# Retuning the order tables of a fused attention and gated MLP kernel: new tables, moved branch hints, a pinned instruction stream and five split stores

## The chip, the cores and the metric

The kernel runs on one core of a Trainium2 chip. The metric is the device time of one execution in microseconds. Before the change three runs took 411.26, 409.59 and 414.25 us, median 411.26 us. The engines are named as in the profile: PE (TensorE), PEld (its weight loads), DVE (VectorE), ACT (ScalarE), POOL (GpSimd) and SP (SyncE, which issues the DMAs here). A name with a q behind it (SPq, PEldq) stands for an engine's sequencer: instructions that aren't counted as busy.

## The reference

Attention over 4 batches, 8 heads, 768 positions, head size 64, with a linear bias per head, a mask that keeps the first 8 keys and the last 96, and then a gated MLP with a mixing step over positions:

```python
scores = scale * np.matmul(q, k.transpose(0, 1, 3, 2)) + bias
scores = np.where(keep, scores, -1000000000.0)     # keep = is_global | is_local
a = softmax(scores);  x = a @ v                    # (B, S, H * D)
h = gelu_tanh(x @ w_in);  u, v = h[..., :512], h[..., 512:]
v_n = (v - mu) / np.sqrt(var + 1e-06) * g_ln
v_s = np.einsum('ts,bsd->btd', w_sg, v_n) + b_sg[None, :, None]
out = x + (u * v_s) @ w_out
```

## The kernel before

**Units.** Attention is cut into 48 units (batch, pair of heads, third of the positions). A unit's work is: load q and k, and v; the scores on PE (line 1104, tile s_ps); bias, maximum, exponential, sum and scaling on DVE, ACT and POOL (lines 1136 to 1166); turning p over; p·v on PE (line 1253, tile av); copying the result to x as a high and a low part. The first 16 units are turned by PE transposes (line 1225, tile tps). From unit 16 on, `turn_blocks` turns them by DVE block transposes (line 1192) and two trips through DRAM: four DMAs far<-tt (line 1200), then one DMA pt<-far (line 1204), which the p·v of that unit waits for.

**MLP.** All MLP matmuls run as three products of high and low parts (lines 570 to 572, tile mm_ps, 128x384 or 128x512 columns). The last batch's output product is done with seven instead of eight block products (`seven`, lines 813 to 815, with DVE sums at line 825 and POOL or DVE sums at line 706). The outputs of the other batches leave by `out_tile`: DVE sum (690), a second sum (692), one store of 128x384 (694).

**Who sets the order.** All these steps are recorded as ops of a `Plan`. Each op may have several ways, that is engines that can run it. Two long strings steer the planner: a digit of `SHIFTS` for each op moves it earlier or later, and a letter of `WAYS` (P, D, A, or - for free) ties it to an engine. `Plan.order` replays the program with a table of costs, and `emit` (line 512) then writes the instructions, each engine's in that order. [...] The planner also knows that PE's instructions come in blocks (`BLOCK, FIRST_BLOCK, FETCH = 256, 194, 4.6`), and where it expects PE to wait early on, `keep_on` (line 507) puts in dummy matmuls on a tile of zeros (line 510, tile on).

**The end.** When all is done, every engine loads a flag (`nc.values_load`, line 1569, TENSOR_LOAD) and branches over a long general path (line 1570, COMPARE_BRANCH) that isn't taken with these inputs. `HINTED` (line 51) names, for DVE and for PE, how many of its ops from the end a BRANCH_PREFETCH_HINT for that branch is put. SP then collects the landings of all stores, and the engines meet at line 1715.

Of the kernel before, what the change touches and what calls it, by code (L numbers as in the profile page):

```python
# [19 lines left out]
P = 128  # L20
B, H, S, D = 4, 8, 768, 64
# [29 lines left out]
HINTED = ("DVE", 40, mybir.EngineType.DVE), ("PE", 14, mybir.EngineType.PE)  # L51
# [12 lines left out]
    "030E00HNf0wWo3NQSa0-F000J3V00-0q00E60u1CCqxzqNK7BSfs0-ebeTiQzPqGhdhU28O-x9np3k-lf-dk-L--HXk9WBg-Mb0OO686YQM1"  # L64
    "e0h0P-yqd---qS8kaDFR5ZV-eCzM-2k04uLgcSrldkZ000q7A00cB00enHlh30xr9cgM-N-OqKsPCYw8qkp0PZy9nokS-R414k0ykpsPavC-"
    "0UfU-JH6Kt-WgQfH1X0gy-yf-jVQd-8NdvjBNKSHS-3982BA7-vDa3Ch2LEFE0rnq2DUFbslTJV4q00t0FMhne9zYT7el9Mty--T1nN-TvLb"
    "NiN0S5m3spkyhWa06hMX07l92859IJH-E-TGd7vZ2i8HVXE8aVdHeVJ4Rhoq61qH9UMyLetgskrIMJe0O-4c0f3n0L5vbOESgBUTarmu49IX"
    "AiWBkaoZ-Twt20X5H7oSiK--0ZAwjXgCndju-YZea--T-P-Zzx7K-O-wCqnwZp0elG7U0e1F0Z7058RnsbddzcHGqRC0l-q0eFCHY1qGiHUn"
    "GQN6Rc1ikjo010KY40V-nWqBOk2WF-S0M6PN08BO0GP1o0vc86-WNa8pfMsSNRG8uqGuEYfaUTok-Kn5GNl8PFtdPcc07q-l4GcgGVsd8-Oy"
    "rsYcaVH2p0900ii0Fj0r00ZIRVy-1-nJ-X1KtksqNrR0SyRfarGro3Zj0SKTNE-wW0JChQOXh-EZ-qA8lTK-H-Rn--0pMBN0a0aLQSuuOBs-"  # L70
    "4U9xGMirD6BR-4FJNxurbhkVT5Y7fiOj2xhlW7CWOs4bTgL3ZMI0WI7ZX04ZCLo5Qy1Tj0wFTqtqfe1Wd0--hv--zcImzro-YZLNQ00YSueM"
    "afZLL-04sOTYHrAGQkMHqhFMvDsud3g0G10rYbouGmZIRsl-aOdDbf9kflwaRmjGGQA4e-fd-YMcgneL--W-zss2yfS03nIrylMX-0XQ03-0"
    "wvFjLmutx-0dIqPJ00fSCE505qlt97zTzcHhTIl77QcSMW6-Tb8SfkCfA-S800mVD8X-cnFZ-HOS-IiSlDpxpFoZQFaRKi-YpwpwIe0fBj2g"
    "08ECdU7OsN40MZpZWn90F10stNQzT3G347V9EZJl0Z00E-DfrD0GQ6pj098kCRliAN-sj3x99nsNmSN40iCEIojpq0nNsjnlFJt006KoCTvP"
    "ZRsC-50UvSAQ8u-nVv-Tp6tiFHtVc0QRk92PTl0C0tOhCjuu0tZ2U0blHB59-H2WXtVucGK--6QoYmqouuyhnppJrra08MLlUBXIIvYD5P0u"
# [12 lines left out]
    "0E2Dun7WTXgBwwkpCGyd"
# [3 lines left out]
    "----P------------P--DA--DD-----------DDA---D----D----------DPA----D--P-ADAD-A-A--------D-DADD--P--D-------DD"  # L92
    "P-------------D-AA-P--P--AD----P--DP----A----------DPAP--P--A--------A--------------A-DDP---D--AD--------P--"
    "-A-D--D-D----------P-A------AD--------DDPDD--D----------P---PA--P--AD--------D-P----A--DDP-P-A----------P--P"
    "P---P------------DADPD----D--------P---DA--D--A----------P-----P--APD-A-A--------D-DPA------DD-----AD-------"
    "---A--A----------P---AA-----AD--P--AD--------D-D------A-D--A-D----------AAPA-P----------P-D----A----------A-"
    "A--P-----------A------A-A-PP-A-D--------P---AA-P------------AD--D--P-----------ADD----------A-D-------------"
    "----AA-P---A--------P-P--P--D--AD------P--D--PD------D------------P-D---------------P-P-----A---P--D--------"
    "--P---AP--D---D--D--PD-P--AP-------------------------A-------------ADD---------A---PP--P-PD-AD-DP-----------"
    "D------D------D------P---------A-ADPDDD--------P-PADD-----------------------AAPPDD--------A-DDDP--DD--------"  # L100
    "-------------D-A---D---------P-A-AP---PDP--------------------------P-A----D--------D--AA---------D--DPP----P"
    "DP-------DPD---------------A-D-A---------D-P-AD----------AD-D----------P-D-----P------------AP--------------"
    "----------A-----------A-PADA----------PPD-----------D-------D-----------D-P-----P---------------------------"
    "----A--D----------A--D-P-----------D-----------DAP-----------------------PPP----------------DD--------------"
# [174 lines left out]
class Plan:  # L279
# [233 lines left out]
    def emit(self, start):  # L513
# [10 lines left out]
        for o in todo:  # L524
# [3 lines left out]
            if o.quarters is not None:  # L528
                self.keep_on(o)
# [1189 lines left out]
```

## Time and profile before

| | |
|---|---|
| three runs, us | 411.26, 409.59, 414.25 |
| the profiled execution, us | 412.14, of which 410.4 us from first to last instruction |
| PE busy | 396.4 us, 97% of the span, 4628 matmuls |
| DVE busy | 349.2 us, 85% |
| ACT, POOL busy | 222.3 us, 54%; 209.4 us, 51% |
| DMA | 67.14 MB, 164 GB/s over the span |

Busy PE isn't PE at its peak: its matmuls overlap, so one that is listed with 0.33 us follows the one ahead by about 0.17 us where nothing holds it. The rows further down are given as the trace's views print them: groups of waits (who waited, for whom, total us, times, longest), timelines (start, duration, engine, line, operation, tiles, and in brackets the idle time ahead and what ended it), single lines of the program with their sequencer instructions, and DMA queues of a stretch.

### The profile page before, as it was taken

To read this page: it belongs to the slowest core of one execution; us is meant where nothing else is said; L and a number is where in the kernel's file an instruction comes from. 1 tells how busy PE (TensorE), PEld (TensorE's weight loads), DVE (VectorE), ACT (ScalarE), POOL (GpSimd) and SP (SyncE) were. 2 spreads that over 40 slices of the span, in tenths; PEclk is the share of its full clock that TensorE was granted. 3 is DMA by queue.
4 is the path that set the end of the run, shared out by engine and by line. 5 is a ranking of instruction groups with operands and counts; after the bars stand their busy time and mean duration, and the time that the engine had idled before them with its cause. 6 is when DMAs were issued, how large, how long until landed. Compare 5 with 4: busy or idle time off the path is not lost.

```text
span 410.4 us, 12613 instructions
## 1 busy us (share of the span) xinstructions
PE 396.4 (97%) x4628; PEld 362.7 (88%) x4630; DVE 349.2 (85%) x1151; ACT 222.3 (54%) x733; POOL 209.4 (51%) x336
## 2 busy tenths in 40 slices
PE   7889999999899999999999999999999999999993
PEld 4777777999799898999999988999999888999993
DVE  7899999999998999987768899986767768796894
ACT  5899999875544777643344575752343324241300
POOL 4434887875544472753121453726113534785780
PEclk9999999999999999999999999999999999999997
DMA  7864765536887787838398566617284641000013
GB/s 244 281 188 145 222 201 149 165 92 176 242 245 262 208 259 199 271 96 260 100 269 270 182 149 197 192 46 227 72 267 106 190 149 58 2 1 2 1 38 122
DMA packets 50035, 67.14 MB, mean 164 GB/s; under 512 B 5808, under 2 KB 33968, under 8 KB 49968
## 3 DMA queue, kind: packets, MB, share of 16 engines
q1 hardware_dynamic: 49968, 66.28, 52.8%
q8 instruction: 38, 0.62, 0.7%
q14 instruction: 29, 0.24, 0.2%
HBM read 47.91 MB, written 18.35 MB: 161 GB/s over the span
## 4 chain that ended last, share of the span: by engine, by line
PE 80%; DVE 10%; DMA 4%; ACT 2%; issue 1%; POOL 1%; SPq 0%; DVEq 0%; ACTq 0%; POOLq 0%
PE mm_ps L570 22%; PE mm_ps L572 21%; PE mm_ps L571 21%; PE av L1253 7%; PE s_ps L1104 6%; DVE p L1136 2%; PE tps L1225 2%; ACT p L1141 1%; DMA pt<-far 1%; DMA far<-tt 1%; DMA stage<-in_w_out_dram 1%; DMA qk<-in_qk_in_dram 1%; DVE win L932 1%; PE mm_ps L815 1%; PE mm_ps L814 1%
## 5 line engine op out<-in xcount | busy, mean ns | idle before, releaser
L1141 ACT ACTIVATE p<-p,pst 128x168 f32<-128x168 f32 (+1 forms) x192 | 80.7, 422 | 34.8 <-DVE pst L1136 30.2
L570 PE MATMUL mm_ps<-wsg,z 128*128 128x384 f32 x192 | 64.9, 338 | 0.0
L572 PE MATMUL mm_ps<-wsg,z 128*128 128x384 f32 x192 | 64.3, 335 | 0.0
L571 PE MATMUL mm_ps<-wsg,z 128*128 128x384 f32 x192 | 64.2, 334 | 0.0
L1163 POOL TENSOR_SCALAR p<-p,pst 128x168 f32<-128x168 f32 (+1 forms) x89 | 39.6, 455 | 36.8 <-DVE pst L1154 30.1
L1136 DVE CUSTOM_DVE_ANT_0 p<-s_ps,bias 128x168 f32<-128x168 f32 (+1 forms) x192 | 54.5, 318 | 4.4 <-PE s_ps L1104 3.2
L1253 PE MATMUL av<-pt,v 64*64 64x128 f32 (+1 forms) x1408 | 48.9, 252 | 4.2 <-DMA far<-tt 1.6
L1253 PEld LDWEIGHTS av<-pt,v 64*64 64x64 f32 x1408 | 37.3, 133 | 13.6 <-issue 7.3
L570 PE MATMUL mm_ps<-x,win 128*128 128x384 f32 x128 | 43.7, 341 | 0.0
L572 PE MATMUL mm_ps<-x,win 128*128 128x384 f32 x128 | 42.9, 335 | 0.0
L571 PE MATMUL mm_ps<-x,win 128*128 128x384 f32 x128 | 42.8, 335 | 0.0
L1104 PE MATMUL s_ps<-qk 64*64 64x64 f32 (+2 forms) x1408 | 39.1, 243 | 0.2 <-DVE vg L592 0.2
L570 PE MATMUL mm_ps<-win,x 128*128 128x512 f32 x96 | 39.2, 408 | 0.0
L572 PE MATMUL mm_ps<-win,x 128*128 128x512 f32 x96 | 37.7, 393 | 0.0
L571 PE MATMUL mm_ps<-win,x 128*128 128x512 f32 x96 | 37.6, 392 | 0.0
L570 PEld LDWEIGHTS mm_ps<-wsg,z 128*128 128x128 f32 x192 | 36.0, 188 | 1.3 <-issue 0.8
L1104 PEld LDWEIGHTS s_ps<-qk 64*64 64x64 f32 x1408 | 34.7, 137 | 2.6 <-issue 1.0
L1141 ACT ACTIVATION_READ_ACCUMULATOR p<-p,pst 128x1 f32 x192 | 36.4, 189 | 0.0
L571 PEld LDWEIGHTS mm_ps<-wsg,z 128*128 128x128 f32 x192 | 36.1, 188 | 0.2
L572 PEld LDWEIGHTS mm_ps<-wsg,z 128*128 128x128 f32 x192 | 36.0, 188 | 0.0
L587 ACT ACTIVATE u<-mm_ps 128x384 f32<-128x384 f32 x32 | 15.6, 488 | 36.5 <-PE mm_ps L572 36.1
L570 PE MATMUL mm_ps<-gt,wout 128*128 128x384 f32 x96 | 32.8, 342 | 0.0
(194 smaller groups left out, 997.6 us busy)
## 6 DMA issues: line engine op xcount, KB each, us to landing
qk<-in_qk_in_dram SPq DMA_DIRECT2D x32, 328.0 KB, 4.5
pt<-far SPq DMA_DIRECT2D x24, 384.0 KB, 4.2
v<-in_v_in_dram SPq DMA_DIRECT2D x32, 256.0 KB, 4.0
out_dram<-o SPq DMA_DIRECT2D x28, 192.0 KB, 3.7
far<-tt SPq DMA_DIRECT2D x52, 96.0 KB, 3.0
qk<-in_qk_in_dram SPq DMA_DIRECT2D x16, 276.0 KB, 3.5
far<-stage SPq DMA_DIRECT2D x44, 96.0 KB, 1.9
v<-in_v_in_dram SPq DMA_DIRECT2D x16, 192.0 KB, 4.0
```

The lines of the kernel that those rows point to most:

```text
L570: mm(ps.ap, ah, bh, start=(i == 0), stop=False)
L571: mm(ps.ap, ah, bl, start=False, stop=False)
L572: mm(ps.ap, al, bh, start=False, stop=(i == n - 1))
L587: op([on_act(n) + (lambda: nc.scalar.activation(out.ap, h.ap, AF.Square, scale=math.sqrt(GELU_C * GELU_A)),)], [h], [out])
L814: mm(ah, bl, start=False, stop=False)
L815: mm(al, bh, start=False, stop=r == 1)
L1104: nc.tensor.matmul(s_ps[h][e * HQ:(e + 1) * HQ, i * W + c0:i * W + c0 + n], qk[rows, qc:qc + HQ], qk[rows, QW + k0:QW + k0 + n], start=Tru ...
L1136: nc.vector.tensor_tensor_reduce(out=p[:, g, cols], in0=s_ps[h][:, i * W:i * W + nk], in1=bias[:, 2 * j + h, w0:w0 + nk], op0=ALU.add, op1 ...
L1141: op([on_act(nk, 0.225) + (lambda p=p, g=g, cols=cols, i=i: nc.scalar.activation(p[:, g, cols], p[:, g, cols], AF.Exp, bias=st[:, 0, i, g: ...
L1163: op([on_pool_ts(nk) + (partial(scaled, lambda o, a, c: nc.gpsimd.tensor_scalar(o, a, c, 1.0, ALU.mult, ALU.mult)),), on_act(nk, 0.13) + ( ...
L1225: nc.tensor.transpose(tps[:, a * P:(a + 1) * P], pc[:, c:c + P], ident)
L1253: nc.tensor.matmul(to, v[rows, vc:vc + D], of, stop=True, skip_group_check=True, **kw)
```

## The change

The two tables are replaced whole. The hints move from 40 to 100 ops before the end on DVE and from 14 to 16 on PE. Ahead of PE's 87th op (counted from 0: `o.place == 86`) an address directive makes the loader pad PE's stream so that the next instruction stands in slot 232 of a 256-slot block; the padding is branched over. Five stores of the third batch (4 of its second half, 1 of its first) are issued as two DMAs of 64 rows each.

```diff
-HINTED = ("DVE", 40, mybir.EngineType.DVE), ("PE", 14, mybir.EngineType.PE)
+IN_TWO = {(B - 2, NCH - 2, KD - 1)} | {(B - 2, NCH - 1, m) for m in range(KD)}
+HINTED = ("DVE", 100, mybir.EngineType.DVE), ("PE", 16, mybir.EngineType.PE)
+ALIGNED = 86, 232
...
 SHIFTS = (
-    "030E00HNf0wWo3NQSa0-F000J3V00-0q00E60u1CCqxzqNK7BSfs0-ebeTiQzPqGhdhU28O-x9np3k-lf-dk-L--HXk9WBg-Mb0OO686YQM1"
+    "LJ0b0XJM0eA0ccV3WXFtrkNLJPNBzF-FhqNNAe2a0eJXbD0C201PKrBnf-6J1QojnW2wfVKTvELgvf1avq45VV30K18Hwfz2OkO5b0dc00ZN"
...
 WAYS = (
-    "----P------------P--DA--DD-----------DDA---D----D----------DPA----D--P-ADAD-A-A--------D-DADD--P--D-------DD"
+    "-----P-D---------D-D-----D---------P-DD-A-DD--A--------------AP----D-D-DAP----A----------PPD-------D------DD"
...
         todo = self.search(start)
+        for i, o in enumerate([o for o in todo if o.quarters is not None]):
+            o.place = i
...
             if o.quarters is not None:
+                if o.place == ALIGNED[0]:
+                    nc.tensor.addr_align(256, offset=ALIGNED[1], max_nops=0)
                 self.keep_on(o)
...
-    def out_tile(self, x, c, m, dst):
+    def out_tile(self, x, c, m, dst, parts=1):
...
-            op([("SP", 0.42, 0.7, lambda: nc.sync.dma_start(dst[ms, cs], o.ap))], [o], [])
+            def store():
+                for h in range(parts):
+                    rows = slice(h * P // parts, (h + 1) * P // parts)
+                    nc.sync.dma_start(dst[m * P + rows.start:m * P + rows.stop, cs], o.ap[rows])
+
+            op([("SP", 0.42, 0.7, store)], [o], [])
...
-                   [[moe.out_tile(x, c, m, dst) for m in range(KD)] for c in range(NCH)])
+                   [[moe.out_tile(x, c, m, dst, 1 + ((b, c, m) in IN_TWO)) for m in range(KD)] for c in range(NCH)])
```

The arithmetic is the same: PE has the same 1620 MLP matmuls, 704 score and 704 p·v products and 88 transposes in both programs, and 105 dummies instead of 106. The line numbers of the changed program are 6 to 11 higher (570 becomes 576, 825 becomes 836, 706 becomes 717).

**First place: PE, the first p·v that is fed through DRAM** (unit 16, tile pt of the far path; x and win are the operands of an MLP product of the v half). Before:

```order
L570 MATMUL mm_ps_1956<-x_989,win_332 128x384
L571 MATMUL mm_ps_1956<-x_989,win_332 128x384
L572 MATMUL mm_ps_1956<-x_989,win_332 128x384
L1253 MATMUL av_2066<-pt_2005,v_1844 64x128
L1253 MATMUL av_2068<-pt_2005,v_1844 64x128 x2
```

Changed:

```order
L576 MATMUL mm_ps_2052<-x_991,win_333 128x384
L577 MATMUL mm_ps_2052<-x_991,win_333 128x384
L578 MATMUL mm_ps_2052<-x_991,win_333 128x384
L1264 MATMUL av_2075<-pt_2006,v_1812 64x128
L1264 MATMUL av_2077<-pt_2006,v_1812 64x128 x2
```

The same p·v follows an MLP product in both, but it has moved six MLP matmuls back: between it and the p·v of unit 15 stood 45 of them and now stand 48, and three more stand ahead of that one (78 for 75).

**Second place: DVE, its last work before the flag is loaded** (o and kept are output tiles of the last batch, mm_ps the last products). Before:

```order
L825 TENSOR_TENSOR o<-x,mm_ps 128x384
L706 TENSOR_TENSOR o<-o,x 128x384
L825 TENSOR_TENSOR o<-x,mm_ps 128x384
L706 TENSOR_TENSOR o<-o,x 128x384
L825 TENSOR_TENSOR kept<-kept,mm_ps 128x384
L1569 TENSOR_LOAD general
```

Changed:

```order
L836 TENSOR_TENSOR o<-x,mm_ps 128x384
L717 TENSOR_TENSOR o<-o,x 128x384
L836 TENSOR_TENSOR kept<-kept,mm_ps 128x384
L836 TENSOR_TENSOR o<-x,mm_ps 128x384
L717 TENSOR_TENSOR o<-o,x 128x384
L1580 TENSOR_LOAD general
```

PE's last product fed `kept`, which takes one DVE instruction; it now feeds an `o`, which takes two.

**Third place: PE, the hint for the branch at the end.** Before:

```order
L572 MATMUL mm_ps_6262<-wsg_1382,z_5928 128x384
L1715 BRANCH_PREFETCH_HINT
L813 MATMUL mm_ps_6052<-x_6240,late_5931 128x384
L814 MATMUL mm_ps_6052<-x_6240,late_5931 128x384
L815 MATMUL mm_ps_6052<-x_6240,late_5931 128x384
```

Changed:

```order
L578 MATMUL mm_ps_6272<-wsg_1381,z_5820 128x384
L1726 BRANCH_PREFETCH_HINT
L576 MATMUL mm_ps_6272<-wsg_1381,z_5937 128x384
L577 MATMUL mm_ps_6272<-wsg_1381,z_5937 128x384
L578 MATMUL mm_ps_6272<-wsg_1381,z_5937 128x384
```

Counted over PE's stream (a weight load and a matmul for each product, scores and p·v issued twice, semaphore waits one each), the hint stood 87 instructions ahead of the branch and now stands 98 ahead. On DVE it stood 49 ahead and now stands 123 ahead.

## Rows read from the trace of the kernel before

**Rows 1.** The page: busy us and share by engine; one instruction queue (packets, MB, share).
```profile
PE 396.4 (97%) x4628; PEld 362.7 (88%) x4630; DVE 349.2 (85%) x1151; ACT 222.3 (54%) x733; POOL 209.4 (51%) x336
...
q8 instruction: 38, 0.62, 0.7%
```

**Rows 2.** Windows: busy us of PE, PEld, DVE, ACT, POOL; clock, DMA share, GB/s.
```profile
100.00:110.00 10.00, 8.37 (x105) 7.91 (x104) 8.86 (x30) 5.72 (x20) 2.67 (x4) 1.00 0.88 264
...
350.00:360.00 10.00, 10.00 (x59) 9.96 (x58) 8.22 (x18) 2.74 (x5) 7.57 (x10) 1.00 0.01 2
```

**Rows 3.** Waits of PE (first, second and last of nine rows).
```profile
PE av L1253 <- DMA far<-tt: 1.6, 1, 1.6
PE av L1253 <- issue: 1.3, 1, 1.3
...
PE s_ps L1104 <- DVE vg L592: 0.2, 1, 0.2
```

**Rows 4.** Timeline of PE around 104 us.
```profile
104.02 0.34 PE L572 MATMUL mm_ps<-x,win 128*128 128x384 f32 x1
105.99 0.68 PE L1253 MATMUL av<-pt,v 64*64 64x128 f32 x24 [1.63 <-DMA far<-tt]
```

**Rows 5.** Timeline of SP's DMA issues, 94 to 101 us.
```profile
94.75 1.79 SPq L1200 DMA_DIRECT2D far<-tt  x4
96.64 2.72 SPq L913 DMA_DIRECT2D stage<-in_w_out_dram  x3
99.68 0.33 SPq L1204 DMA_DIRECT2D pt<-far  x1
```

**Rows 6.** Timeline of PE around 17 us.
```profile
17.12 0.43 PE L1253 MATMUL av<-pt,v 64*64 64x128 f32 x2 [1.26 <-issue]
```

**Rows 7.** Chain of waits, a stretch of attention: start, us, engine, tile, line.
```profile
200.09 1.06 PE av L1253 x48
201.15 1.18 PE s_ps L1104 x64
```

**Rows 8.** Timeline of the end.
```profile
403.13 0.56 DVE L825 TENSOR_TENSOR o<-x,mm_ps 128x384 f32<-128x384 f32 x1
...
403.73 0.56 DVE L706 TENSOR_TENSOR o<-o,x 128x384 f32<-128x384 f32 x1
403.73 0.34 PE L815 MATMUL mm_ps<-gt,wout 128*128 128x384 f32 x1
404.20 0.55 DVE L825 TENSOR_TENSOR kept<-kept,mm_ps 128x384 f32<-128x384 f32 x1
```

**Rows 9.** Line 1570, the branch: ns min/median/max, first and last start us.
```profile
L1570 SPq EVENT_SEMAPHORE  x8: 17/17/17, 405.7 to 408.2; - x8
...
L1570 DVEq COMPARE_BRANCH  x1: 84/84/84, 404.7 to 404.7; - x1
L1570 SPq COMPARE_BRANCH  x1: 53/53/53, 405.2 to 405.2; - x1
L1570 PEldq COMPARE_BRANCH  x1: 3664/3664/3664, 405.6 to 405.6; - x1
L1570 DVEq EVENT_SEMAPHORE  x1: 21/21/21, 408.0 to 408.0; - x1
```

**Rows 10.** Line 1715, hint and closing of the program, the same columns.
```profile
L1715 SPq EVENT_SEMAPHORE  x10: 17/28/825, 408.2 to 410.3; - x10
...
L1715 PEldq BRANCH_PREFETCH_HINT  x1: 45/45/45, 393.8 to 393.8; - x1
```

**Rows 11.** DMA from 393.8 to 405.6 us, its only instruction queue.
```profile
q14 instruction: 2, 0.02, 0.4%
```

**Rows 12.** DMA from 405 to 408.2 us: PE's instruction queue; last store's landing.
```profile
q8 instruction: 1, 0.02, 2.2%
...
out_dram<-kept SPq DMA_DIRECT2D x1, 192.0 KB, 3.0
```

**Rows 13.** DMA from 400 to 404.7 us: landing of the store of kept before it.
```profile
out_dram<-kept SPq DMA_DIRECT2D x1, 192.0 KB, 2.0
```

More of the change, by code (lines that the diff above doesn't have):

```diff
@@ new lines @@
+    "MZWw9n4-oUxuckTXWIeThmq5IKlV-50O4VtS-j0dmo94U2mZ000JHtHns-xfD4QQ67J64jZ0F57R00w4vodyM8eh09s0Do35X4F16SE1ntVO"
+    "E-u4KT46E5V0ZUb8woA8RJU6RMrB0Vup-Z6rQ80doSPV5ur----8--yTKZ-t---n--v2BBt7oj00000Y4R5m5hNUzCuRldRjts7x-g-yT-nv"
+    "9iQ1WZku8ml8bnSe0LswyuV0z1--l7y--C2mg--M5q--pWcx9i9V04iBLAzpTIE0Pb16sjtanFsWclFX9GLMHSZEJJKgGdI5k2-Rtjk84hMy"
+    "Nr5-sPpQ-75vtIGtFFTtUrxdGbrY-KYrfadRvcS8rqlWGiWDDU3bJRJL5qz0bvcvvxxaDrt3PFRDAtRuupblR-vJQJ7uFRrmXd00M3eWtF2f"
+    "1p1L23GVp18LmG4Ys1OccgKJ-h1-RBC16u8f3Y1Y-bDM-67ER5PZSI0NhhBDSRC9w3Q6aagO9l-Scgpw-Lj8YCw1crW1wl-eKRq7-sQeRx5m"
@@ new lines @@
+    "lFGV0ayIU5NIsUa4XNtouxHb-X0Kd3510YAcf6NB69jpSJW-smSAw0g0awTSdOVzdAZ49eaQYVaFFF68EeJYH-ubr0Bd0XWca0g-I9-F0-13"
+    "16P04LPKt0w0FG160wsfiUuT-k-k7eGgZW-lcDTj8u-6qi9M3QY1F0Qlm0LoO0005038BzvdGsvT450-t--Zr--f---y-y-V-qjdUsONBnS3"
+    "G9dWv-c9fU-mW0l6TlptOJX3NR-d-Oa-9NkWAOeKA6DBBgL4AABDAkFG4WpyGwaocSO-esWFHQ0O8Dccnk04rlQzmHWhYQUz-S8U0BHU07yK"
+    "3krSIbGr--B7Okc-zdywZf0Z004kkA9WykrfGAfcWeWPL5Fm0OMVntcDhr069fJXhwosU2o0nxT9M9Yzrz-P-UzVfYdcvJL1CCG-1NSrOTvr"
+    "d-UJshGqmYK6vJ-0Lv00f1PmjjImM1OoNNe7Bh8CJnCd0okgfs3h80Osh100nilYA9Cc7A-6bYWRMgF0SiUFBePOyz-w-qrnJFr--O-M7Xhj"
@@ new lines @@
+    "sUIhtF5FiG7F0T0wFt-vyWQa2Nq6skk30907DS2v09Og595u0FMa06ym8MkGj5GVKtBpvaQaXEsyTTUO80-tucRXtf9P430-7H1F-Aa90k0R"
+    "f88Z-WwNGp---tPqbo-----5WomDz--8jCMP7CSyMvUYOccyudtpidAJcFdEUpWdbLMBgDtbo-fgdXEc0Ft-5FcU0fylFQ5-Z-vhl---f---"
+    "maHh000qvp7XuSs00MFWpv3c60uj4zoNAhllFQiGeCIf7LEM3fSBGNYE3aX9E00cnV9-8n-PViI4LfA9oUQwsfLK1Gu69XJLez-100UUVSg0"
+    "kfhetJ2V0t2aSiT0gvtR--zq-I-s--Rt-C8Y5T-7jPpDxxJqYDVkXS4bkuR7203c--bKsnje9aeSgHHSNm0vK03452G50N3lDQoCnPWR8nvC"
+    "gr30ezB-8d7Bv01S0oXFQW00MaDnPIsdr-rYSsdUS4ajTCY5XmVe--vks6WglA0-ym-lO0c0ymoAzVV1PRTL-0N831c-kFnW79N9aNrR0FqA"
@@ new lines @@
+    "5H9o7fKNaMfJMDHVS00AaEUW9-6QSIaWe0i2XrVracVWKgYoIQJZ070TyywyyWbmBQxyA-lVD-5af2U5k0q50010aZee0ejFjNbLGy77kSHF"
+    "7M11zEBd9CNjDH6KwLEKtG6Rp-L5-z26kI4J70SE1JU50s20P0eTE8SowcRo-rr-z-oz-EcOUYS-1Ix0IKlR6G4-BqlLWcP-C0Td1RPp000p"
+    "UhEOr5gqeFG4urFP00YOOZ2glpPsO6S0hH4ilc5a4h5Glzlw-w---NaWDx---vWUfj--jgB--o85M8T78--jhf72PW9Xk0saVT91LJobMO5u"
+    "BGTxIV-MvCCUMO5PFdCPhXW-CftbZd55N7977QMfiDQocd0B0SEQPCnwAGstW8gKtft3ptE7hHN8ezE-jUbrkIvi6HfRX0LFycVaJFfC-CTI"
+    "dkknY8ndEP1Yt0MkLtb0ahHVpsxN8sy8Zbg65AG-r7Ie-I-s6PS2p-0cRUOaW5S2-cbguayZH828d1Fj---yXt--bU9X5jmAF--c0DviNbNe"
@@ L89 @@
+    "Uu-VGwkZO-L-EII-UeGSLd0S6pps-MdaRMbJJ-UKf02902bv-Z67vOBH0bHuzuvrZYmKpmKbnWyQs0xCxEWh5lFcHLE0X2V8K5A29308qGEu"
+    "i087I-Q7j-Z7PdxtSt1alYoBiUa4ZElKzmIS0IKTW0pk9UOSO0vfKNiR7T-IcmTGxuC0jbukopGLeofaeWEWZMbsWsH00000-nG0Db0008lC"
+    "kyQarbqijX5u9PFqWJuSlbBMlVl4I1BkJttKO2BQHMhJ3oNxu8YCgKIBG005JNHEcxt9GabMMLnHq20xlaakpx3T8TwFK3yDbO-lxf54UytL"
+    "-G4V7OYo-eTvzcFMsY-Z"
 )
 WAYS = (
[L92 removed]
@@ L117 @@
+    "-P--P-PP---P-D-----------------------P-----------------DPPD---------------DAD---------------D-DD---P---P----"
+    "-----------DDDD-DDA--------D---------------D-DPAP-A------------D---D--------P--DD-------PDPP-D--------------"
+    "-----D----D---------"
 )
```

69 lines of the change are left out of this document (21 added, 48 removed).

## The prediction

> **What bounds the kernel now.** I began with the page. PE is busy for 97% of the span and nothing else is above 85% [rows 1], so the question is where PE's missing time lies, and what stands behind its last matmul. The windows answer the first half: from 110 us to the end of the matmuls PE has no idle stretch worth naming, and a typical window, 350 to 360 us, holds 59 matmuls in 10.00 us, one per 0.17 us, at the full clock [rows 2]. The one bad window behind the start is 100 to 110 us, with 8.37 us busy. The waits of PE name it: nine rows, 7.4 us in all, the largest a p·v that waits 1.6 us for the trip through DRAM, then 1.3 us in which PE waited for nothing but its own instructions [rows 3]. The timeline shows the first: a matmul starts at 104.02, the p·v of unit 16 at 105.99 [rows 4]. SP had put three weight loads between the four DMAs out (94.75) and the one back (99.68) that fills its tile [rows 5]. The second lies at 17.12 us, in dense attention [rows 6].
>
> The end is the other place. The last matmul starts at 403.73 and DVE is done at 404.75 [rows 8], yet the span is 410.4 us. The rows of line 1570 say why: PE's branch, which should take tens of ns, took 3,664 ns, and DVE, whose branch was over at 404.8, did nothing until 408.0 [rows 9]. SP spent 825 ns of its closing sequence on the last arrival, PE [rows 10]. PE's instruction queue moved 38 packets of 16 KB for some 9,260 matmuls and weight loads, about 250 instructions each [rows 1]; none of them came between the hint at 393.8 [rows 10] and the branch at 405.6 [rows 11], and one came right behind the branch [rows 12]. So the hints of the old program prefetched nothing; DVE's was no better.
>
> **The change part by part**, against the profiled run's 412.14 us (410.4 us of span and 1.74 around it; it lies 0.88 above the median 411.26, and I move the sum over to the median at the end).
>
> *PE's own work* is unchanged: same matmuls, one dummy fewer. Changes between quarter-array and whole-array matmuls go from 40 to 42; both new ones are in the first 30 us, where dummies fill PE's waits. 0.0.
>
> *The wait at 104 us.* Six more MLP matmuls stand ahead of this p·v, 6 x 0.17 = 1.0 us of work that used to come behind the wait. SP's rows there keep their order (four DMAs out, three weight loads, one back) and DVE has one instruction fewer ahead of the second block transpose, so the landing hardly moves. I take -1.0. Bounds: 0 if the landing slips as far, -1.6 if the wait goes whole [rows 4].
>
> *The other waits of PE* (7.4 less these 1.6, less 1.3 for instructions and 1.0 for the first tile of zeros) come to 3.5 us; the 1.1 us for the first softmax stays, since the order there is the same. Every engine's order around the others is new. They could go (-2.4), or a new one could come as long as the longest row (+1.6) [rows 3]. With no row for the new order I take 0.
>
> *The alignment.* PE meets one branch over some 70 pads, at a place ahead of a group of dummies. A branch whose target is at hand costs SP 0.5 us from its start (405.2) to the next instruction (405.7) [rows 9]; behind waiting dummies that is hidden. 0, at most +0.5. It also moves the block edges of all that follows; see the third rival.
>
> *The split stores.* Five more DMA issues on SP of 0.3 us each, at about 345 to 370 us, where the DMA share is 0.01 [rows 2] and SP only waits for the next output. No load is queued behind them. 0; if the buffers came free 0.4 us later, no PE op would see it there.
>
> *The hints.* PE's stood 75 instructions ahead of its last block edge (counted at 194 + 256k, which puts the idle time of [rows 6] at the 450th instruction, on an edge) and is now 8 ahead of it, with 90 more to the branch; the old branch came 12 behind its edge. DVE's stood behind its last edge and is now just ahead of it. If the target is fetched when the edge frees a block, PE's 3.66 us go. But DVE's and PE's late arrival cover each other and the last store: it landed 3.0 us after its issue [rows 12], where the one of the same size before it took 2.0 [rows 13], and SP's closing could start no earlier. What PE alone adds is SP's 825 ns less the usual 28 [rows 10]: -0.8, taken. Bounds: 0 if the hints still miss; -1.9 if, with no fetch in its way, the last store also lands 1.0 us sooner, plus a tenth from the next arrival.
>
> *The tail.* PE's last product now feeds an o tile instead of kept, two DVE instructions instead of one. In the trace such a pair starts at 403.13 and 403.73, 0.60 apart, and ends 0.56 later; the single one takes 0.55 from 404.20 [rows 8]. DVE would end at 404.20 + 0.60 + 0.56 = 405.36 instead of 404.75, and the last store, the flags and the branches with it: +0.6. Nothing covers it.
>
> Sum: -1.0 - 0.8 + 0.6 = **-1.2 us**, 410.9 for the profiled run, **410.1 us** against the median.
>
> [...] The rows show a branch that waited 3.66 us for its target in spite of a hint [rows 9]. [...]
>
> **The rivals.**
> 1. *The hints miss again.* For it: neither old hint brought a packet in, and PE's too had an edge between it and the branch [rows 10 and 11]. Against it: the old edge lay only 12 instructions ahead of the branch. The end then keeps its 3.66 us: -1.0 + 0.6 = -0.4, 410.9 us.
> 2. *The waits ahead of 110 us go, and the last store lands early.* -1.6 - 2.4 - 1.9 + 0.6 = -5.3, 406.0 us. For it: all of it is in the list of waits. Against it: the order of every engine is new there, and what makes one wait go can make the next.
> 3. *Slower: PE outruns its instruction fetch at a moved edge.* Attention matmuls run at 1.18/64 us (scores) and 1.06/48 us (p·v) each [rows 7], two of each to a product. Between two edges near 200 us the changed stream now holds 27 score products, 32 p·v products and 6 MLP matmuls: 1.0 + 1.4 + 1.0 = 3.4 us, with the changes of array shape 3.7. Before, the shortest block behind the start held 32, 24 and 14: 1.2 + 1.1 + 2.4 = 4.6 us, and PE showed no idle time there. A fetch asked for on arrival took 3.66 us [rows 9]. So this block stands at the point where it decides: a fetch slower than about 3.7 us stalls PE. One more block, near 295 us, has 32, 25 and 11: 4.2 us. If both stall like the one at 17 us, 1.3 each [rows 6], the forecast becomes -1.2 + 2.5 = +1.3, 412.6 us.
>
> **How the numbers follow.** Forecast 0.45 (410.1, by its own bounds 408 to 412), rival 1 0.25 (410.9), rival 2 0.13 (406.0), rival 3 0.17 (412.6). The predicted time is the forecast's, 410.1. The range: the first two cases lie within 408 to 412.5, rival 3 with one more wait of 1.0 reaches 413.4, and half of rival 2 comes in at 407.0; beyond these ends I leave about 2 in 10. One per cent is 4.1 us, about what separates a change from none in runs that spread from 409.59 to 414.25; below 407.1 lies most of rival 2 and a little of the forecast's tail, 0.14; above 415.4 only rival 3 with a new wait of 1.6 and more, 0.06; the rest, 0.80, is within 1%.
>
> **What would show it.** In the changed profile: PE's COMPARE_BRANCH well under 1 us and an instruction packet between its hint and its branch (else rival 1); the idle time ahead of the first p·v from DRAM at about 0.6 us instead of 1.63; DVE's last pair ending about 1.3 us after PE's last matmul ends; PE's "issue" row no longer than 1.3 us in all (rival 3 shows as PE idle on "issue" near 200 and 295 us). The forecast is wrong if new waits of over 1 us stand in PE's list, or if the last matmul doesn't start within 402 to 404 us.

## The result, and the profile after

The changed kernel takes **406.92 us** (median of 6 runs, 406.4 to 409.24) against 411.72 us for the kernel before (6 runs, same chip): ratio 0.9895, interval 0.9849 to 0.9942, 4.3 us by the ratio. That is just below the low end of the range (407.0) and 3.2 us below the predicted time. The profiled execution of the changed kernel took 406.97 us, its span is 405.2 instead of 410.4.

The 5.2 us of span lie in two places: the last matmul starts at 400.23 instead of 403.73 (-3.50), and the stretch from there to the end is 4.96 instead of 6.63 us (-1.67). First PE. The page (busy us, share, instructions), and the windows of [rows 2]:

```profile
PE 396.0 (98%) x4629; PEld 362.8 (90%) x4629; DVE 345.5 (85%) x1149; ACT 224.9 (56%) x736; POOL 198.9 (49%) x335
...
q8 instruction: 38, 0.62, 0.7%
```

```profile
100.00:110.00 10.00, 10.00 (x114) 9.58 (x113) 9.51 (x35) 5.45 (x23) 4.13 (x5) 1.00 0.81 259
...
350.00:360.00 10.00, 10.00 (x60) 10.00 (x59) 8.39 (x18) 4.30 (x9) 7.82 (x9) 1.00 0.00 1
```

PE's work is the same, and the bad window, 8.37 us busy before, is full. The list of PE's waits (total us, times, longest), whole:

```profile
PE tps L1236 <- POOL p L1174: 2.3, 2, 1.4
PE s_ps L512 <- DVE on L976: 1.0, 1, 1.0
PE av L1264 <- ACT pt L1241: 0.5, 2, 0.4
PE tps L1236 <- DVE p L1177: 0.4, 1, 0.4
PE tps L1236 <- PE av L1264: 0.2, 1, 0.2
```

4.4 us instead of 7.4 [rows 3]. Neither the trip through DRAM nor "issue" is among them; the waits that are left all lie within the first 30 us. Without the first tile of zeros they sum to 3.4 us; the same kind of rows came to 3.5 before. PE's timeline at the first p·v from DRAM, which waited 1.63 us in [rows 4]:

```profile
104.31 0.34 PE L578 MATMUL mm_ps<-x,win 128*128 128x384 f32 x1
104.57 0.68 PE L1264 MATMUL av<-pt,v 64*64 64x128 f32 x24
```

No bracket: nothing to wait for. SP's rows of the trip, answering to [rows 5]:

```profile
93.19 1.80 SPq L1211 DMA_DIRECT2D far<-tt  x4
95.75 2.15 SPq L924 DMA_DIRECT2D stage<-in_w_out_dram  x3
98.08 0.33 SPq L1215 DMA_DIRECT2D pt<-far  x1
```

The trip leaves 1.56 us earlier (93.19 for 94.75), and the DMA back is issued at 98.08 for 99.68, so it follows the first DMA out by 4.89 us, much as before (4.93). By the landings in the trace, the DMA back has landed at 102.24 instead of 105.85, 4.2 us behind its issue instead of 6.2: 2.3 us ahead of the p·v, where it had been the last to come.

Then the end. The timeline, answering to [rows 8]:

```profile
400.23 0.34 PE L826 MATMUL mm_ps<-late,wout 128*128 128x384 f32 x1
400.68 0.55 DVE L836 TENSOR_TENSOR o<-x,mm_ps 128x384 f32<-128x384 f32 x1
401.26 0.56 DVE L717 TENSOR_TENSOR o<-o,x 128x384 f32<-128x384 f32 x1
```

The pair of DVE sums ends 1.59 us after the start of the last matmul; the single sum ended 1.02 after it. The branch and the closing (ns min/median/max, first and last start), answering to [rows 9, 10]:

```profile
L1581 SPq EVENT_SEMAPHORE  x8: 17/17/17, 402.7 to 403.8; - x8
...
L1581 DVEq COMPARE_BRANCH  x1: 84/84/84, 402.2 to 402.2; - x1
L1581 SPq COMPARE_BRANCH  x1: 53/53/53, 402.2 to 402.2; - x1
L1581 PEldq COMPARE_BRANCH  x1: 387/387/387, 402.5 to 402.5; - x1
L1581 DVEq EVENT_SEMAPHORE  x1: 21/21/21, 402.8 to 402.8; - x1
```

```profile
L1726 SPq EVENT_SEMAPHORE  x10: 17/28/28, 403.9 to 405.1; - x10
...
L1726 PEldq BRANCH_PREFETCH_HINT  x1: 45/45/45, 390.0 to 390.0; - x1
```

PE's branch takes 387 ns for 3,664, DVE goes on 0.6 us after its branch for 3.3, and no closing semaphore of SP waits any more (28 for 825 ns). The DMA of 391.0 to 392.5 us has PE's instruction packet behind the hint (it starts at 391.24, 1.25 us after it), which [rows 11] lacked; the DMA from 401.8 us has the last store, 1.9 us for the 3.0 of [rows 12]:

```profile
q8 instruction: 1, 0.02, 5.4%
```

```profile
out_dram<-o SPq DMA_DIRECT2D x1, 192.0 KB, 1.9
```

### The profile page after: what moved, and what is told of

It is laid out like the page before. It is cut to its first block, busy times and chain, and to the rows that moved or that the text cites. A ratio compares the mean times of both kernels' runs of the same rounds, so it can differ in the third digit from the quotient of the medians.

```text
span 405.2 us, 12620 instructions
## 1 busy us (share of the span) xinstructions
PE 396.0 (98%) x4629; PEld 362.8 (90%) x4629; DVE 345.5 (85%) x1149; ACT 224.9 (56%) x736; POOL 198.9 (49%) x335
## 4 chain that ended last, share of the span: by engine, by line
PE 88%; ACT 5%; DVE 4%; issue 1%; DMA 1%; POOL 0%; DVEq 0%; ACTq 0%; POOLq 0%
PE mm_ps L576 24%; PE mm_ps L578 23%; PE mm_ps L577 23%; PE av L1264 8%; PE s_ps L1115 6%; ACT p L1152 2%; PE tps L1236 2%; DVE p L1147 1%; PE mm_ps L826 1%; PE mm_ps L825 1%; PE mm_ps L824 1%; ACT p L1172 1%; DMA ni<-in_n_gl_dram 1%; ACT pt L1241 1%; ACT stage L927 1%
```

## The experiments

Every run is set against the kernel before on the same chip; ratios are to it. "End stretch" is the time from the end of DVE's last sum to the end of the span: 5.61 us before, 3.37 in the changed kernel.

### The parts of the change, one by one

**e1_tables**: the new tables alone.

```diff
-HINTED = ("DVE", 100, ...), ("PE", 16, ...)
+HINTED = ("DVE", 40, ...), ("PE", 14, ...)
-ALIGNED = 86, 232
+ALIGNED = -1, 0
-IN_TWO = {(B - 2, NCH - 2, KD - 1)} | {(B - 2, NCH - 1, m) for m in range(KD)}
+IN_TWO = set()
```

> The new tables alone: the hints stand at 40 and 14 as before, no alignment, whole stores. Theory A (part of the gain is not order but where PE's instruction blocks begin and what their fetches run into): the end is as before, PE's branch about 3.7 us and DVE silent for 3 us, which costs 2.0 to 2.5 us against the changed kernel, and a PE fetch falls near 95 us into the trip of unit 16 through DRAM again, one of its 16 landings about 1.4 us late; the order has about 2 us of room there, so PE waits 0 to 0.5 us. Time about 409.3 us where the changed kernel has 406.9 and the old one 411.7. Theory B (order alone): the wait at 104 us stays away, PE's last matmul starts as early as in the changed kernel (400.2 us), the landing isn't late; time about 409.2 us. The times are alike; the late landing tells them apart.

Measured 408.09 us (before 410.74), ratio 0.9944 (0.9928 to 0.9961). The last matmul starts at 399.71, the wait at 104 us is gone, DVE's pair ends 1.59 after the last matmul's start. Its end stretch is 4.77. Both theories had the time 1.2 us too high: A failed at the branch, and B failed too, for one landing of the trip is late (table below). Line 1581 of this kernel:

```profile
L1581 DVEq COMPARE_BRANCH  x1: 84/84/84, 401.4 to 401.4; - x1
...
L1581 PEldq COMPARE_BRANCH  x1: 490/490/490, 402.0 to 402.0; - x1
...
L1581 DVEq EVENT_SEMAPHORE  x1: 21/21/21, 404.7 to 404.7; - x1
```

PE's old hint *hits* here (490 ns for 3,664), though it was not moved: by the counts, the new tables alone shift PE's stream by six instructions against the block edges. DVE's misses (3.3 us from its branch to its next row).

**e2_align**: old tables, old hints, whole stores, the alignment alone. **e3_align_hints**: the same with the new hints.

```diff
+ALIGNED = 86, 232            # both, beside the old SHIFTS and WAYS
-HINTED = ("DVE", 40, ...), ("PE", 14, ...)
+HINTED = ("DVE", 100, ...), ("PE", 16, ...)      # e3 only
```

> The old tables and old hint places with the alignment alone. PE's last block edge now lies 82 instructions ahead of the branch and the old hint 5 ahead of that edge; DVE's hint stands where it failed. Theory A: the PE fetch that ran at 97 us moves away from the trip of unit 16, its landing comes 1.4 us earlier and PE's wait at 104 us falls from 1.6 to under 0.4 us; PE's branch takes under 0.5 us, DVE's is still silent for 3 us, the end gains 0.5 to 1.0. But the alignment puts 32 score and 31 p.v products between two edges near 200 us, 2.6 us of work against a fetch of 3.7 us: PE should stand idle there for about 1 us on nothing but issue. Sum -1.3 - 0.8 + 1.0 = -1.1, about 410.6 us. Theory B: the wait at 104 us stays at 1.6 us, since no order has changed; with the end's gain about 410.9 us, or 411.9 if the block stalls.

> The old tables with the alignment and the new hint counts (100 and 16); on PE the hint stands 17 ahead of the last edge, on DVE 9 or so. Against the run with the alignment alone only the end should change: both branches under 0.5 us, the last store landing about 2 us after its issue instead of 3, the end 2.0 to 2.5 us shorter than in the old kernel. Theory A: -1.3 at 104 us, +1.0 at 200 us, -2.3 at the end: about 409.1 us. Theory B: -2.3 at the end alone, about 409.4, with the wait at 104 us still 1.6.

Measured 409.26 us, ratio 0.9965 (0.9951 to 0.9978), and 408.76 us, 0.9950 (0.9925 to 0.9975). With the tables unchanged, the wait at 104 us falls from 1.6 to 0.2 us in the first and is out of the list in the second. PE's branch takes 391 and 387 ns. The stall near 200 us that a short block was to bring appeared in neither. Between the two DVE's hint hits, and the end stretch goes from 4.61 to 4.10; the intervals overlap, so in time that half microsecond is not shown.

**e4_whole**: the changed kernel with whole stores (`IN_TWO = set()`).

> The changed kernel with the five stores whole again. Both theories: no change, 406.9 +- 0.4 us; DMA is all but idle there. If the parts matter (say by moving SP's stream so that its own fetch misses the last store), the last store lands later than 2 us after its issue and the time is 0.5 to 1 us longer.

Measured 406.89 us, ratio 0.9922 (0.9904 to 0.9940). In time the split stores cannot be told from nothing. The end stretch is 3.90, though, and e12 below says why.

In this set the tables give 2.65 us, alignment with hints 1.98, both together 3.85 (410.74 less 406.89). In the profiles they overlap: either alone removes most of the wait at 104 us, and either alone makes PE's hint hit. In time the overlap is 0.8 us, which the intervals do not separate from none.

### What made the wait at 104 us

The landings of each DMA are in the trace, 16 for each. In the kernel before, 15 of the 16 landings of the second to fourth far<-tt come together (96.75 to 97.02, 97.23 to 97.52, 97.73 to 97.99), and one of each at 99.10, 99.29 and 99.52; the DMA back goes out at 99.68. A packet of PE's instructions starts at 96.77. That was the new theory (C): the packet holds up one landing of each DMA it meets. Five runs move the packet (e5, e6, e9, e10, e11).

The late landing was not all that held the DMA back. SP's first weight load behind the four DMAs out, which was being issued when the packet came, took 1.63 us to issue, where SP's usual issue takes 0.43 (the median over all traces):

```profile
96.64 1.63 SPq L913 DMA_DIRECT2D stage<-in_w_out_dram  x1
```

The third load was issued by 99.36, only 0.16 us ahead of the last landing (99.52). So with every landing on time and this issue still held, the DMA back could have gone out hardly earlier.

**e5_offset122** and **e6_offset156** (more on their hints below):

```diff
-ALIGNED = 86, 232
+ALIGNED = 86, 122            # e5;  86, 156 in e6
```

> The changed kernel with one number changed: the stream is aligned to 122 instead of 232, so that every block edge of PE behind 62 us comes 110 instructions later. Two things follow. (1) At the trip through DRAM of unit 16: in the changed kernel PE's instruction packets start at 88.5 and 103.3 us and the trip lies between them; 110 of 256 instructions later the first falls at 88.5 + 14.8 x 110/256 = 94.9 us, into the four DMAs out (93.2 to 94.5 issued). Theory C (the instruction packet takes one of the 16 DMA engines and holds up the one landing of each DMA that uses it): one of the 16 landings of one or more of these DMAs comes 1.1 to 1.8 us behind the other 15. Its rival (packets do not get in each other's way; the late landing in the kernel before had another cause): all 16 land within 0.3 us, as in the changed kernel. By both, no time is lost here, since SP issues three weight loads until 98.1 ahead of the DMA back. (2) At the end: the hint now stands at slot 138 of a block and the branch at slot 236 of the same one, no edge between. Theory A (the hinted block is fetched when the next edge frees a place): PE's branch takes about 3.6 us again instead of 0.39, the span ends 4.1 to 5.0 us after the last DVE instruction instead of 3.4, and the time is 407.7 to 408.5. Rival B (a hint fetches its target by itself): an instruction packet within 2 us of the hint, the branch under 0.5 us, the time as the changed kernel's, 406.9.

> The changed kernel aligned to 156 instead of 232: edges 76 instructions later, the hint 84 ahead of the last edge and the branch 14 behind it, nearly as in the kernel before (75 ahead, 12 behind), where the hint missed; in the run with the new tables alone it was 68 ahead and 18 behind, and hit. Theory A (any edge between hint and branch is enough): an instruction packet some 7.5 us after the hint, the branch under 0.5 us, time 406.9. Rival D (the branch must not come too soon behind the edge, and 14 is too soon): the branch takes about 3.6 us, the span ends 4.1 to 5.0 us after DVE's last instruction, time 407.7 to 408.5. PE's packet near the trip of unit 16 moves from 88.5 to about 92.9 us, just ahead of the first DMA out: theory C expects at most the first of them with a late landing, by 0.7 us or less.

Measured 407.16 us, 0.9902 (0.9871 to 0.9932), and 407.03 us, 0.9894 (0.9864 to 0.9924). Neither trip came out as theory C had expected: in e5 the packet came at 95.8, behind the last landing, and delayed none; in e6 the fourth DMA's landing was 1.78 us late, where at most 0.7 on the first was expected.

**e9_old_offset116**: e3 with the edges moved so that a packet falls into the trip again.

```diff
-ALIGNED = 86, 232
+ALIGNED = 86, 116            # old SHIFTS and WAYS, whole stores
```

> The old tables and whole stores with the new hints, as in the run of alignment and hints, but aligned to 116 instead of 232: block edges of PE behind 62 us come 116 instructions later. With 232 PE's packets lay at 89.1 and 105.2 us around the trip of unit 16 (issued 94.5 to 95.8, back 98.2) and PE did not wait at 104. Now one falls at 89.1 + 16.1 x 116/256 = 96.4 us, as in the kernel before (96.77). Theory C (the packet delays the one landing of each DMA out that shares its DMA engine, the DMA back is issued only behind the last landing, and the first p.v waits for it): one landing of two or three of the four DMAs comes 1.1 to 2.1 us behind the others, the DMA back is issued 3.3 to 3.7 us behind the last DMA out instead of 2.3, and PE is idle 0.8 to 1.8 us ahead of its first p.v from DRAM; time 409.6 to 410.3 against the 408.8 of the run with 232. Rival (that wait went because the padding and the calmer start moved PE against SP, not because of the packet): landings may scatter, but the p.v does not wait, 408.8. At the end hint and branch lie in one block: by the run with 122 the hint should still hit at once.

Measured 409.90 us, ratio 0.9973 (0.9954 to 0.9992): by the ratios 0.9 us behind e3, which the intervals do not separate; the trace does. First row of its list of PE's waits, and SP's rows of the trip:

```profile
PE av L1264 <- DMA far<-tt: 1.9, 1, 1.9
```

```profile
93.95 3.67 SPq L1211 DMA_DIRECT2D far<-tt  x4
97.73 1.33 SPq L924 DMA_DIRECT2D stage<-in_w_out_dram  x3
99.25 0.33 SPq L1215 DMA_DIRECT2D pt<-far  x1
```

The wait is back, and longer than in the kernel before (1.6). The four DMAs out take SP 3.67 us to issue instead of 1.80, and the DMA back follows the first DMA out by 5.3 us (by chance also 3.67 in e3). The first DMA out alone (stretch 93.9 to 94.2 us; the last number is from issue to last landing), then the second (94.3 to 94.6), then the packet (95.2 to 95.6):

```profile
far<-tt SPq DMA_DIRECT2D x1, 96.0 KB, 1.8
```

```profile
far<-tt SPq DMA_DIRECT2D x1, 96.0 KB, 4.0
```

```profile
q8 instruction: 1, 0.02, 29.0%
```

The second met the packet: 4.0 us for 1.8. What decided here, though, was the fourth DMA out. SP was issuing it when the packet came, and the issue took 2.33 us (0.46 in e3):

```profile
95.29 2.33 SPq L1211 DMA_DIRECT2D far<-tt  x1
```

So its 16 landings came together, but at 98.83 to 99.07, behind both late ones (98.34 and 98.58); the weight loads were through at 99.06, and the DMA back went out at 99.25. Of theory C, then, the late landings and the wait came as expected; that a late landing is what the DMA back waits for did not hold here. Over all kernels, "late" being the landing that comes behind the other 15 of the same DMA:

| kernel | PE's packet, us | far<-tt issued | late landings, us late | PE's wait at 104 |
|---|---|---|---|---|
| before | 96.77 | 94.75 to 96.08 | 2nd 2.08, 3rd 1.77, 4th 1.53 | 1.6 |
| e9 | 95.4 | 93.95 to 95.29 | 2nd 2.10, 3rd 1.87 | 1.9 |
| e1 | 95.5 | 92.65 to 94.00 | 4th 1.78 | none |
| e6 | 94.6 | 92.12 to 93.46 | 4th 1.78 | none |
| e11 | 96.2 | 93.66 to 95.00 | 4th 1.87 | none |
| e10 | 95.6 | 92.74 to 94.08 | none | none |
| e5 | 95.8 (all landed 95.41) | 92.17 to 93.51 | none | none |
| after, e2, e3, e4, e7, e8, e12 | none from 90 to 102 | | none | 0.2 in e2, else none |

Of six packets that fell into the trip five delayed landings, by 1.5 to 2.1 us; in e10 one that began 0.1 us ahead of the fourth DMA's first landing did not. Counted over the far<-tt DMAs of all 14 traces, the last landing came over 1 us behind the other fifteen in 196 of the 486 that met a packet of PE ahead of their fifteenth landing, and in 21 of the 1306 that met none. SP's long issues are tied to the packets more closely still: of the 181 DMA issues of SP that took over 1 us, 178 were under way when a packet of PE ended, and were done 0.14 to 0.42 us (median 0.37) behind its end.

From the first DMA out to the landing of the DMA back the trip took 11.1 us in the kernel before and in e9, 9.7 in e2 and 8.9 in e3, and 9.1 to 10.1 in the kernels with the new tables. From the first DMA out to the moment when PE came to the p·v it was 9.3 to 9.6 us with the old tables and is 11.1 to 11.7 with the new. So two things, each enough by itself, all but remove the wait: the packet out of the trip's way, or a trip that leaves earlier against PE; with the new tables the delays of e1, e6, e10 and e11 cost nothing. There the DMA back follows the first DMA out by 4.9 us even where no packet is near, for SP waits ahead of its three weight loads (0.5 to 0.7 us each in the changed kernel, for DVE and POOL). That the DMA back itself lands faster in the changed kernel (4.2 us for 6.2) is a third part; why is not shown. Why one landing in 16 is hit, the records do not tell either.

Moving the edges has a side effect in e5, e6, e9, e10 and e11: by the count of its instructions, their padding reaches across a block edge, and the branch over it takes 1.23 to 1.91 us instead of 0.19 to 0.20. PE's idle time behind it was 0.4 us at most (0.26 in e9), too little for e9's wait.

### When a hint works

e5 and e6 kept both hints and moved the edges. In e5 hint and branch lie in one block, and theory A (an edge must lie between) expected a miss. It hit: 372 ns, with the packet in the stretch from 389.3 to 391.8 us:

```profile
q8 instruction: 1, 0.02, 3.2%
```

The packet starts at 390.4, 1.1 us behind the hint. In e6, with the edge 84 instructions behind the hint, it starts 7.1 us behind the hint, and hits too (453 ns). So an edge between hint and branch is not needed for a hit; where one lies 84 instructions behind the hint, the packet comes 6.0 us later than in e5. What lets the packet come at either moment is not shown.

**e10_offset154**, **e11_offset146**: the branch 12 and 4 instructions behind the last edge.

```diff
-ALIGNED = 86, 232
+ALIGNED = 86, 154            # e10;  86, 146 in e11
```

> The changed kernel aligned to 154 instead of 156, so that the branch comes 12 instructions behind the last edge, exactly as counted in the kernel before, where the hint missed; with 14 it hit. Theory D' (the branch must stand more than 12 or 13 instructions behind the edge): PE's branch about 3.6 us, no instruction packet between the hint and the branch, span 4.1 to 5 us behind DVE's last instruction. Rival (the edge that frees a place is enough, however close; the old miss had another cause): a packet about 7 us behind the hint and a branch under 0.5 us.

> The same with 146: the branch 4 instructions behind the last edge. Theory D': a miss, PE's branch about 3.6 us. Rival: a hit, under 0.5 us, since PE's sequencer waits for DVE between the edge and the branch and so leaves the packet 3 us and more.

One time each: 407.28 and 409.60 us. e10 hits (453 ns), its packet 8.9 us behind the hint. e11 misses; between its hint and its branch (390.5 to 402.6 us) there is no packet of PE's queue, and the branch and the closing are:

```profile
L1581 PEldq COMPARE_BRANCH  x1: 4007/4007/4007, 402.7 to 402.7; - x1
L1581 DVEq EVENT_SEMAPHORE  x1: 21/21/21, 403.0 to 403.0; - x1
```

```profile
L1726 SPq EVENT_SEMAPHORE  x10: 17/28/2392, 404.1 to 407.7; - x10
```

With 4 instructions it missed and with 12 it hit, in one run each; no run lies between. The kernel before missed with 12, but that count came from a fitted first edge and can be off by a few; whether it really stood closer stays open. DVE's hint hit here, and the end stretch is 5.70, no shorter than without either hint (5.60 in e7 below): with PE late, DVE's hint gave nothing here.

**e7_no_hints**: the changed kernel without the call that places the hints.

```diff
-            if o in hinted:
-                self.tc.mark_branch_hint_location("general", engines=(hinted[o],))
```

> The changed kernel without either hint; everything else, the alignment too, as it is. What the two hints give in all. By the prediction's own step (the hints give 0.8 us, at most 1.9): PE's branch 3.6 us, DVE's next instruction 3.2 us behind its branch, the last store with one late landing (1.0 us behind the others), the span ending 4.2 to 5.6 us after DVE's last instruction instead of 3.4; time 407.7 to 409.0, the last matmul unmoved. Rival (an aligned end needs no hint, the placing of the edges alone gives the gain): branch under 0.5 us, time 406.9.

Measured 409.34 us, ratio 0.9948 (0.9929 to 0.9968), 2.2 and 2.3 us more than the runs with hints beside it (e5, e6), a little over the range expected. Branch, closing, and the first of PE's waits:

```profile
L1579 PEldq COMPARE_BRANCH  x1: 3912/3912/3912, 403.7 to 403.7; - x1
```

```profile
L1724 SPq EVENT_SEMAPHORE  x10: 17/28/1242, 405.2 to 408.6; - x10
```

```profile
PE av L1262 <- issue: 2.1, 1, 2.1
```

The end stretch is 5.60, so the hints are worth 2.2 us. Two more rows of this run matter, the instruction packet in the stretch from 391.5 to 393.5 us and the landing of the last store:

```profile
q8 instruction: 1, 0.02, 4.1%
```

```profile
out_dram<-o SPq DMA_DIRECT2D x1, 192.0 KB, 2.1
```

A packet comes at the last edge, 392.1 us, without any hint, and the branch misses all the same. So a packet ahead of the branch, the sign that the prediction named, does not tell a hit by itself; the branch's own time does. And the late landing of the last store, which was expected here, did not come: 2.1 us without hints, 1.9 with them. What the hints give here is the time that SP waits for DVE's flag (0.9 us) and PE's (1.24).

The row of PE's waits is something else: the "issue" stall of [rows 6]. Up to there the streams of the changed kernel, e5, e7, e10, e11 and e12 agree, and the stall is 0, 0, 2.1, 0.35, 1.45 and 0.9 us. It varies from execution to execution, roughly with the moment PE's first packet comes (from 13.6 us in e5 to 15.7 in e7; but 13.9 with 0.35 in e10 and 14.1 with none in the changed kernel), and is as large as most of the spread of the runs (406.4 to 409.24).

### The last half microsecond

**e12_six_parts**: one more store split.

```diff
-IN_TWO = {(B - 2, NCH - 2, KD - 1)} | {(B - 2, NCH - 1, m) for m in range(KD)}
+IN_TWO = {(B - 2, NCH - 2, KD - 2), (B - 2, NCH - 2, KD - 1)} | {(B - 2, NCH - 1, m) for m in range(KD)}
```

> The changed kernel with one more store of the block before in two parts, six instead of five, so that SP issues one DMA more some 40 us before the end. SP's DMAs take eight semaphores in turn, and at the end SP waits for them in a fixed order. With whole stores the last store is on the third of them, and the span ends 1.76 us behind its landing (traces of before's stores in four kernels: 1.76 to 1.77, the wait for PE's flag left out); with five more DMAs it is on the eighth, and the span ends 1.40 behind it. Theory E (the five split stores gain 0.36 us through this turn, and by nothing else): one DMA more puts the last store on the first semaphore, SP goes through the seven others after its landing, at 0.07 to 0.10 us each, and the span ends 1.9 to 2.0 us behind the landing, 0.5 to 0.6 later than the changed kernel's. Rival (the split stores gain by coming sooner, or the 0.36 has another cause): 1.4 us again, or 1.76.

One time: 407.6 us. DVE ends at 401.82 and the last store lands at 403.89, nearly as in the changed kernel (401.82, 403.79), but the span ends at 405.82, 1.93 behind the landing instead of 1.40. Branch and closing:

```profile
L1581 SPq EVENT_SEMAPHORE  x8: 17/17/17, 403.9 to 404.4; - x8
```

```profile
L1726 SPq EVENT_SEMAPHORE  x10: 17/28/28, 404.5 to 405.8; - x10
```

All eight semaphores come behind the landing here; in the changed kernel seven of the eight are done before it (402.7 to 403.3). Theory E holds in the profiles: the split stores gain 0.36 us by what they do to the count of SP's DMAs. In time, with one run here and none to tell in e4, it is not shown.

**e8_tail**: the sum of x's two halves for the last tile is made by POOL ahead of time.

```diff
+        one, two, sum_of_x, plus_ps = self.tail        # o<-x,mm_ps and o<-o,x
+        todo.remove(two)
+        one.way, two.way = (*one.way[:-1], plus_ps), ("POOL", *two.way[1:3], False, 0.0, sum_of_x)
+        todo.insert(1 + max(i for i, o in enumerate(todo) if o.way[0] == "POOL"), two)
```

> The changed kernel with another tail, to win back what the prediction put down as the tail (+0.6): the sum of x's two halves for the last output tile is made by GpSimd some 2 us earlier, and one VectorE instruction adds the last product to it, instead of two behind the last matmul. Nothing else moves (one TENSOR_TENSOR more on GpSimd behind its last one, one fewer on VectorE). If VectorE's pair behind the last matmul sets the end: VectorE ends 0.56 earlier, 1.0 us after the start of the last matmul instead of 1.59; the time falls by 0.5 to 406.4. Rival (SP's chain of closing stores and flags, or PE's last instruction, sets it): under 0.2 us gained. Worse only if GpSimd's sum comes too late: it should start about 397.8 and take 1.2, ending 1.7 us before it is needed.

Measured 406.84 us (406.05 to 408.0), ratio 0.9893 (0.9867 to 0.9919), the lowest median of its set. The timeline, POOL's, PE's and DVE's last rows:

```profile
398.29 1.21 POOL L883 TENSOR_TENSOR o<-x 128x384 f32<-128x384 f32 x1
```

```profile
400.63 0.34 PE L830 MATMUL mm_ps<-late,wout 128*128 128x384 f32 x1
```

```profile
400.50 0.55 DVE L840 TENSOR_TENSOR kept<-kept,mm_ps 128x384 f32<-128x384 f32 x1
401.07 0.56 DVE L884 TENSOR_TENSOR o<-o,mm_ps 128x384 f32<-128x384 f32 x1
```

DVE ends 1.00 us behind the last matmul's start instead of 1.59, and the span 4.49 behind it instead of 4.96. The gain is in the profile as expected; beside e5 and e6 the time is 0.2 to 0.3 lower, which the intervals do not separate.

## Why the prediction was right or wrong

The terms against the two profiled executions, us:

| step of the prediction | predicted | measured | where |
|---|---|---|---|
| PE's own work | 0 | -0.5 | the rest of PE's 3.5, behind no listed wait |
| the wait at 104 us | -1.0 | -1.6 | went whole |
| the other waits of PE | 0 | -0.1 | 3.5, now 3.4 |
| the "issue" row, left out of the sum | none | -1.3 | not in this execution |
| the alignment | 0 | 0 of its own | no stall near 200 or 295 us |
| the split stores | 0 | -0.36 | closing semaphores |
| the hints: PE's flag | -0.8 | -0.8 | 825 to 28 ns |
| the last store's landing, priced with the hints | 0 (bound -1.0) | -1.08 | 3.0 to 1.9 behind its issue |
| the tail | +0.6 | +0.57 | DVE's pair |
| sum | -1.2 | -5.2 | |

**Right**: that the wait at 104 us and the branch were the places that count; that the new hints hit; that the other waits of PE come to nothing in sum; the price of PE's flag and of the tail, both to within 0.1; and that no PE work changed. Rival 1 fell (387 ns), and so did rival 3: blocks short enough to decide by its sum stalled nowhere; why is not shown. That it counts where a hint stands, as the forecast took it, the runs bear out: PE's branch took 3,664 ns with the old hints, 387 with the new and 3,912 with none (e7).

**Wrong in size.** By its own signs the forecast failed: the last matmul was to start within 402 to 404 us and started at 400.23, and the wait for the first softmax, which was to stay at 1.1 us, is now 1.4 (for POOL instead of ACT). The time that came, 406.9, is nearest rival 2 (put at 0.13, 406.0), but partly by luck. Of that rival's terms the wait at 104 us went and the last store came early; the 3.5 us of other waits, its largest term, stayed. In their place went a row that neither the forecast nor the rival counted.

- *The wait at 104 us.* The step that failed is that "the landing hardly moves". It moved by 3.6 us (105.85 to 102.24): 1.6 because the trip left earlier and 2.0 because the DMA back took 4.2 us instead of 6.2. The step had read SP's three weight loads between the DMAs out and back [rows 5] as a fixed order; that one of them was held for 1.63 us, and one landing of each of three DMAs out was late, both beside PE's instruction packet, it did not see. e9 brings that wait back with another alignment alone. The alignment, costed at nothing, and the tables each take it away.
- *The "issue" row.* The forecast took it as it stood. e7, e10, e11 and e12 show it to come and go between executions of the same stream (where it is 1.5 and 2.1, the wait for POOL behind it is 1.9 instead of 2.3). It was in the profiled execution of before and not in that of after; most of it is chance, no gain. That also helps to put the profiles' difference, 5.2, above the 4.3 of the ratio.
- *The last store.* The step on the hints took its late landing as given, and its -1.0 for an end of the range only. It went: in the kernel before, that store's sixteenth landing came at 407.80, 1.1 us behind the other fifteen, beside instruction packets at 406.2 to 406.8 [rows 12]. That these packets delayed it, as at 104 us, and that the hints took the delay away, is argued: without hints e7's store was on time.
- *The split stores.* They were priced as issues on an idle queue. That they shift which of SP's semaphores the last store gets was not thought of.
- *PE's 0.5 us* behind no listed wait stays open.

The ends of the range come out of no sum that is shown: rival 3 with one more wait of 1.0 gives 413.6, not 413.4, and none gives 407.0, which the result just missed.

## What to carry to other kernels

Here 178 of SP's 181 DMA issues of over 1 us were under way when a packet of PE's instructions ended, and of the 217 far<-tt DMAs whose last landing came over 1 us late 196 had met one. Where one landing of sixteen is late, or one DMA issue takes over 1 us, at a place that decides, look at the instruction queues' packets beside it, and move the block edge or the transfer. A missed branch at the end costs what is exposed behind it, here 0.8 us of it where the last store was late too (before) and 2.2 where it was not (e7); read it against the last store's landing, not against the other engines' branches. And before a "waited for nothing" row of one execution is put into a sum, see whether it is in another execution of the same program.

## What the runs showed of the hardware

- In both kernels PE's queue moved 38 packets of 16 KB, about 250 instructions each. With the alignment moved, the packet near the trip came at 95.8, 94.6 and 95.4 us, where blocks of 256 instructions had put it at 94.9, 92.9 and 96.4 (e5, e6, e9). The planner's 4.6 us for a fetch is a number of its model; in the runs a missed branch took 3.66 to 4.01 us.
- With hint and branch in one block, a packet of PE started 0.9 and 1.1 us behind the hint (e9, e5); with an edge 84 and 86 instructions behind the hint it started 7.1 and 8.9 us behind it (e6, e10). With the branch 4 instructions behind that edge no packet came ahead of the branch and it took 4,007 ns (e11); with 12 one did, and it took 453 (e10).
- Without a hint a packet of PE came at the last edge too, and the branch still took 3,912 ns (e7).
- Where instruction packets of PE (16 KB, 1.1 to 1.9 us by their own records) fell into the trip of unit 16, one of the 16 landings of a DMA came 1.5 to 2.1 us late, in five of six kernels.
- A DMA issue of SP that was under way at such a packet lasted until 0.38 us behind the packet's end in the kernel before and in e9: 1.63 and 2.33 us for a usual 0.43.
- SP goes through its closing semaphores in a fixed order at 0.07 to 0.10 us each: the span ended 1.40, 1.76 or 1.93 us behind the last landing, by which of the eight the last store was on.
- The branch over the padding took PE 0.19 to 0.20 us in seven kernels, and 1.23 to 1.91 us in the five whose padding reaches, by the count, across a block edge.
